# Column-tiled mask, sums and memory selection, an output projection of 512 columns and a Pm in two parts, in a recurrent attention kernel

## Chip, cores and metric

One core of one Trainium2 chip. The metric is the device time of one execution in microseconds (us); lower is better. "Faster" or "slower" is claimed at 2%. All runs here were with a granted TensorE clock of 0.996 to 0.999 of full speed. In the profiles PE is TensorE's matmuls, PEld its weight loads, ACT the scalar engine, DVE the vector engine and POOL GpSimd. Where two kernels are compared, they ran in the same call on the same chip; "ratio" is the mean time of a kernel's fast runs over the mean time of the other's fast runs of the same rounds, so it is not quite the ratio of the medians quoted beside it.

## The reference, cut to what matters

A memory-augmented attention goes through a sequence in 64 segments of 32 rows. Each segment sees 8 memory rows and its own 32 rows, and the first 8 rows of its output are the next segment's memory. So the 64 steps form a chain. (A channel MLP, independent of it, is mixed in at the end.)

```python
for s in range(64):                                   # n_seg
    h = concat([mem, x[:, 32*s:32*s+32]], axis=1)     # 8 + 32 rows, 512 wide
    q, k, v = (einsum('btd,dhe->bhte', h, W) for W in (Wq, Wk, Wv))   # 32 heads of 128
    scores = where(mask, einsum('bhqe,bhke->bhqk', q, k) * scale, -1e9)
    o = einsum('bhqk,bhke->bhqe', softmax(scores), v)
    o = einsum('bhte,hed->btd', o, Wo)                # to 512
    mem = o[:, :8]                                    # the chain
    outs.append(o[:, 8:])
```

## The kernel before

The kernel runs four steps per group of 128 rows of x. I call a step's place in its group its **quarter**, 0 to 3. In each step TensorE makes Q, K, V of the segment (`qk_unit`, `v_unit`), scores, sums for the softmax, the product of the memory rows (`Pm`), the output projection of them (`wo_unit`, together with the previous step's x rows, which lag behind), the mask of the next step, the product of the x rows (`Px`), and the selection of the new memory from the projection's result `wsb`. (`UTT` is the product copied out of PSUM for the projection; `hT` holds the next step's input, transposed.) Between them stand units of *fill*: matmuls of other work (`run_fill`). Eight units of fill are used in quarters 0 to 2: five behind the sums, one before the projection, two behind the selection. In quarter 3 the units are six, one, two *before* the selection and one behind it.

Most of these matmuls use a quarter of the array's columns (`tile_position=(0, 32*j)`): four with different j run side by side. The two products use a quarter of the rows (`(32*j, 0)`). Sums, mask and selection use the whole array.

```python
def mask_mm():
    B = bank(7, [P, 512])
    S = B[:, 0:NG * EW].rearrange("p (i e) -> p i e", e=EW)
    nc.tensor.matmul(S, lhsT=ident[:], rhs=MkA[:].unsqueeze(2).to_broadcast([P, 4, 2, EW]), start=True, stop=True, ...)
    return B, S

def wo_unit(bk, ut, c0, u, d0=0, d1=Dm):
    for (j, i) in HORD[4 * u:4 * u + 4]:
        g = i % 4
        nc.tensor.matmul(bk[32 * g:32 * g + 32, :], lhsT=ut[:, i, j, c0:c0 + 32], rhs=Wo_sb[:, 4 * i + j, d0:d1],
                         start=(j == 0 and i < 4), stop=(j == 3 and i >= NG - 4), tile_position=(0, 32 * g))

# --- in step s, after Q, K, V and scores (cut) ---
nc.scalar.activation(out=E[:, :, 0:16], in_=S[:, :, 0:16], func=ACTF.Exp, scale=scale, accum_out=hist[:, s, 0:1])
nc.scalar.activation(out=E[:, :, 16:EW], in_=S[:, :, 16:EW], func=ACTF.Exp, scale=scale, accum_out=hist[:, s, 1:2])
sm = bank(nc_, [P, NG, 8])
nc.tensor.matmul(sm[:], lhsT=BO[:], rhs=E[:, :, 8:16], start=True, stop=False)
nc.tensor.matmul(sm[:], lhsT=BO[:], rhs=E[:, :, 0:8], start=False, stop=True)
...
run_fill(5 + (si == 3))
nc.vector.reciprocal(out=R[:, 0:8 * NG]..., in_=sm[:])
nc.vector.tensor_tensor(out=Pm..., in0=E[:, :, 0:16]..., in1=R[:, 0:8 * NG]..., op=ALU.mult)      # 128 columns
av(Um, 8, s, V, Pm, 8, 0, 0)                         # 32 matmuls on Pm[.., 8:16], then 8 on Pm[.., 0:8]
nc.tensor.matmul(sr, lhsT=BO[:], rhs=E[:, :, 16:48], ...)                  # row sums, into bank 7
nc.tensor.matmul(sr[:, :, 24:32], lhsT=BO[:], rhs=E[:, :, 48:56], ...)
for j in range(4):                                   # UTT, by ACT and DVE in turn
    (nc.scalar.copy if j % 2 else nc.vector.tensor_copy)(out=UTT[..., j, ...], in_=Um[j][:])
nc.vector.reciprocal(out=R[:, 8 * NG:]..., in_=sr)
run_fill(1)
for half in range(2):
    d = slice(256 * half, 256 * half + 256)
    wp = bank((nb, nd)[half], [P, 256])
    for u in range(8):
        wo_unit(wp, UTT[Tp % 2], 24 - 8 * sp, u, 256 * half, 256 * half + 256)
    ...
    (nc.scalar.copy if half else nc.vector.tensor_copy)(out=wsb[:, d], in_=wp[:])
S_next = mask_mm()
av_x(s - 1, (ne, na, nc_, nb))                       # the Px product
run_fill(2 * (si == 3))
for m in range(KC):                                  # selection of the new memory
    nc.tensor.matmul(aT[:, m, :], lhsT=wsb[:, m * P:(m + 1) * P], rhs=Sel[:, 0:M], start=False, stop=True, ...)
nc.vector.tensor_copy(out=hn[:, :, 0:M], in_=aT)     # hT of the next step; its Q waits for this
for _ in fill: pass
```

Of the kernel before, what the change touches and what calls it, by code (L numbers as in the profile page):

```python
# [23 lines left out]
def kernel(ctx, tc, A_x, A_mem0, A_Wq, A_Wk, A_Wv, A_Wo, A_seg_len, B_x, B_w1, B_b1, B_w2, B_b2, gate_w, out):  # L24
# [327 lines left out]
    def prep_q(s):  # L352
        T, si = divmod(s, SPT)
        nc.gpsimd.tensor_copy(out=QT[:, :, 32:40], in_=QL[T % 2][:, :, LEFT * si:LEFT * si + LEFT])

    def mask_mm():

        B = bank(7, [P, 512])
        S = B[:, 0:NG * EW].rearrange("p (i e) -> p i e", e=EW)
        nc.tensor.matmul(S, lhsT=ident[:], rhs=MkA[:].unsqueeze(2).to_broadcast([P, 4, 2, EW]),  # L360
                         start=True, stop=True, skip_group_check=True)
        return B, S

    def scores(S, s, i0, i1):
# [232 lines left out]
    def run_fill(n):  # L597
        for _ in range(n):
            next(fill, None)
# [21 lines left out]
    for s in range(nseg + 2):  # L621
        T, si = divmod(s, SPT)
        live = s < nseg
        hc, hn = hT[s % NHT], hT[(s + 1) % NHT]
        if live:
            fill = side_work(T, si)
        if si == 1 and T + 2 < NT:
            x_load(T + 2)
        if si == 3 and T + 1 < NT:
            left_v_in(T + 1)  # L630
        if si == 3 and T + 2 < NT:
            x_left(T + 2)
        if live:
            B, S = S_next
            na, nb, nc_, nd, ne = ring
            ring = (nd, ne, na, nc_, nb)
            qk_banks = (na, nb, nc_, nd, ne)
            if s >= 2:
                ux_out(s - 2)
                flush(act_q)  # L640
            if s + 1 < nseg:
                prep_h(s + 1)
            if s >= 1:
                prep_q(s)
                x_mul(s - 1)
            flush(dve_q)
            BANKS = [(0,) + HF[0], (1,) + HF[0], (0,) + HF[1], (1, H // 2, 3 * H // 4), (1, 3 * H // 4, H)]
            for bi, (t, h0, h1) in enumerate(BANKS):
                bk = bank(qk_banks[bi], [P, 512])
                for kc in range(KC):  # L650
                    qk_unit(bk, hc, t, h0, h1, kc)
                Tv = qk_tr(bk, h0, h1)
                dst = QT[:, h0:h1, 0:32] if t == 0 else KT[:, h0:h1, :]
                (nc.gpsimd.tensor_copy if bi == 2 else nc.scalar.copy)(out=dst, in_=Tv)  # L654
            V = cw.tile([P, NG, Dh], BF16, tag="V", name="V")
            Vs[s] = V
            vb0, vb1 = bank(na, [P, 512]), bank(nb, [P, 512])
            for kc in range(KC):
                v_unit(vb0, hc, 0, kc)
            nc.scalar.copy(out=v_out(V, 0), in_=vb0[:])  # L660
            flush(dve_q, 9)
            scores(S, s, 0, 3 * NG // 4)
            v_unit(vb1, hc, 1, 0)
            scores(S, s, 3 * NG // 4, NG)
            for kc in range(1, KC):
                v_unit(vb1, hc, 1, kc)
            E = cw.tile([P, NG, EW], BF16, tag="E", name="E")
            R = cw.tile([P, NG * 40], FP32, tag="R", name="R")
            Es[s], Rs[s] = E, R
            nc.scalar.activation(out=E[:, :, 0:16], in_=S[:, :, 0:16], func=ACTF.Exp, scale=scale, accum_out=hist[:, s, 0:1])  # L670
            nc.scalar.activation(out=E[:, :, 16:EW], in_=S[:, :, 16:EW], func=ACTF.Exp, scale=scale, accum_out=hist[:, s, 1:2])
            sm = bank(nc_, [P, NG, 8])
            nc.tensor.matmul(sm[:], lhsT=BO[:], rhs=E[:, :, 8:16], start=True, stop=False)  # L673
            nc.tensor.matmul(sm[:], lhsT=BO[:], rhs=E[:, :, 0:8], start=False, stop=True)  # L674
            nc.scalar.copy(out=v_out(V, 1), in_=vb1[:])
            run_fill(5 + (si == 3))
            nc.vector.reciprocal(out=R[:, 0:8 * NG].rearrange("p (i q) -> p i q", q=8), in_=sm[:])  # L677
            Pm = cw.tile([P, NG, 16], BF16, tag="Pm", bufs=1, name="Pm")
            nc.vector.tensor_tensor(out=Pm[:].rearrange("p i (a q) -> p i a q", q=8), in0=E[:, :, 0:16].rearrange("p i (a q) -> p i a q", q=8),  # L679
                                    in1=R[:, 0:8 * NG].rearrange("p (i q) -> p i q", q=8).unsqueeze(2).to_broadcast([P, NG, 2, 8]), op=ALU.mult)  # L680
            Um = [bank(k, [P, NG, 8]) for k in (nd, ne, na, nc_)]
            av(Um, 8, s, V, Pm, 8, 0, 0)
            sr = B[:, 0:NG * 32].rearrange("p (i q) -> p i q", q=32)
            nc.tensor.matmul(sr, lhsT=BO[:], rhs=E[:, :, 16:48], start=True, stop=False, skip_group_check=True)  # L684
            nc.tensor.matmul(sr[:, :, 24:32], lhsT=BO[:], rhs=E[:, :, 48:56], start=False, stop=True, skip_group_check=True)
            Tp, sp = divmod(s - 2, SPT)
            for j in range(4):
                (nc.scalar.copy if j % 2 else nc.vector.tensor_copy)(out=UTT[Tp % 2][:, :, j, 24 - 8 * sp:24 - 8 * sp + M], in_=Um[j][:])  # L688
            nc.vector.reciprocal(out=R[:, 8 * NG:].rearrange("p (i q) -> p i q", q=32), in_=sr)  # L689
            run_fill(1)  # L690
        else:
            if s == nseg:
                ux_out(s - 2)
                x_mul(s - 1)
                av_x(s - 1, (ne, na, nc_, 7))
            else:
                ux_out(s - 2)
            flush(dve_q)
            Tp, sp = divmod(s - 2, SPT)
        wsb = cw.tile([P, Dm], BF16, tag="wsb", bufs=9, name="wsb")  # L700
        for half in range(2):
            d = slice(256 * half, 256 * half + 256)
            wp = bank((nb, nd)[half], [P, 256])
            for u in range(8):
                wo_unit(wp, UTT[Tp % 2], 24 - 8 * sp, u, 256 * half, 256 * half + 256)
            if half == 0:
                flush(act_q, 2)
            (nc.scalar.copy if half else nc.vector.tensor_copy)(out=wsb[:, d], in_=wp[:])  # L708
        if s >= 2:
            wsbs[s] = wsb  # L710
        if s + 1 < nseg:
            S_next = mask_mm()
        if live and s >= 1:
            av_x(s - 1, (ne, na, nc_, nb))
        run_fill(2 * (si == 3))
        if s + 1 < nseg:
            aT = S_next[0][:, NG * EW:NG * EW + KC * M].rearrange("p (k m) -> p k m", m=M)
            for m in range(KC):
                nc.tensor.matmul(aT[:, m, :], lhsT=wsb[:, m * P:(m + 1) * P], rhs=Sel[:, 0:M], start=False, stop=True, skip_group_check=True)  # L719
            nc.vector.tensor_copy(out=hn[:, :, 0:M], in_=aT)  # L720
        for _ in fill:
            pass
# [142 lines left out]
```

## Time and profile before

| | before |
|---|---|
| time, median (lowest to highest) | 835.51 us (835.13 to 835.79, 4 runs) |
| one step, median by quarter | 10.94, 11.03, 11.21, 11.46 us |
| end of V to Pm product, by quarter | 1.46, 1.46, 1.50, 1.68 us |
| Pm product to selection | 3.38, 3.38, 3.38, 3.93 us |
| selection to the next Q | 0.63, 0.63, 0.63, 0.54 us |
| Q to end of V | 5.47 to 5.54 us |
| TensorE instructions in the program | 48,500 |

The table divides a step by starts of TensorE's matmuls (medians over the 52 steps from the third group of four to the fifteenth, from the single records of the trace; the end of V is the start of its last matmul plus 0.206). A step is a chain on TensorE, so what a part loses or gains by this table is what the kernel loses or gains. The lines on which this rests are in the prediction.

### The profile page before, as it was taken

To read this page: it belongs to the slowest core of one execution; us is meant where nothing else is said; L and a number is where in the kernel's file an instruction comes from. 1 tells how busy PE (TensorE), PEld (TensorE's weight loads), DVE (VectorE), ACT (ScalarE), POOL (GpSimd) and SP (SyncE) were. 2 spreads that over 40 slices of the span, in tenths; PEclk is the share of its full clock that TensorE was granted. 3 is DMA by queue.
4 is the path that set the end of the run, shared out by engine and by line. 5 is a ranking of instruction groups with operands and counts; after the bars stand their busy time and mean duration, and the time that the engine had idled before them with its cause. 6 is when DMAs were issued, how large, how long until landed. Compare 5 with 4: busy or idle time off the path is not lost.

```text
span 832.9 us, 49239 instructions
## 1 busy us (share of the span) xinstructions
PE 804.7 (97%) x22405; PEld 495.4 (59%) x22417; DVE 501.7 (60%) x1019; ACT 434.0 (52%) x1245; POOL 273.7 (33%) x625
## 2 busy tenths in 40 slices
PE   6999999999999999999999999999999999999886
PEld 4665555665666665566566556656656656665554
DVE  5764256565666566666656565656656665666553
ACT  3555544555455555555554555455555555555552
POOL 8000234242424333332424242434243243424220
PEclk9999999999999999999999999999999999999999
DMA  9791210100000010101010100000010101010000
GB/s 318 253 391 44 87 32 7 28 12 24 15 23 23 17 28 10 37 11 35 10 27 13 35 11 22 23 20 26 12 34 10 36 10 35 5 35 5 10 5 24
DMA packets 38216, 37.64 MB, mean 45 GB/s; under 512 B 13545, under 2 KB 36434, under 8 KB 36466
## 3 DMA queue, kind: packets, MB, share of 16 engines
q1 hardware_dynamic: 37874, 34.31, 12.4%
q8 instruction: 177, 2.90, 1.5%
q14 instruction: 37, 0.30, 0.1%
q0 software_dynamic: 128, 0.13, 0.1%
HBM read 26.03 MB, written 6.29 MB: 39 GB/s over the span
## 4 chain that ended last, share of the span: by engine, by line
PE 93%; DVE 3%; DMA 1%; issue 1%; SPq 1%; ACT 1%; DVEq 0%; ACTq 0%
PE b L211 35%; PE b L233 18%; PE b L222 17%; PE b L384 5%; PE hp L456 4%; PE bp L473 4%; PE b L360 2%; PE b L369 2%; PE b L684 2%; PE b L719 1%; PE b L389 1%; PE b L673 1%; DMA Wo_sb<-in_A_x_dram 1%; PE b L320 1%; PE b L373 0%
## 5 line engine op out<-in xcount | busy, mean ns | idle before, releaser
L217 DVE STREAM_TRANSPOSE Tt<-b 128x512 f32<-128x512 f32 (+1 forms) x384 | 225.6, 613 | 85.5 <-PE b L211 71.8
L211 PEld LDWEIGHTS <-hT 128*32 128x32 bf16 x5120 | 134.7, 97 | 100.0 <-DVE hT L720 15.4
L233 PE MATMUL b<-Wo_sb,UTT 128*32 128x256 bf16 (+1 forms) x4736 | 162.7, 285 | 1.2 <-ACT UTT L619 0.8
L222 PE MATMUL b<-Wv_sb,hT 128*32 128x512 bf16 x2048 | 141.9, 379 | 0.0
L211 PE MATMUL b<-Wq_sb,hT 128*32 128x512 bf16 x2048 | 132.9, 380 | 1.4 <-DVE hT L720 1.4
L211 PE MATMUL b<-Wk_sb,hT 128*32 128x256 bf16 (+1 forms) x3072 | 133.3, 308 | 0.0
L233 PEld LDWEIGHTS <-UTT 128*32 128x32 bf16 x4736 | 121.4, 97 | 19.1 <-ACT UTT L619 1.5
L654 ACT CAST KT<-Tt 128x256 bf16<-128x256 f32 (+1 forms) x192 | 87.1, 476 | 53.6 <-DVE Tt L217 53.6
L605 POOL TENSOR_TENSOR Px<-E,R 128x256 bf16<-128x256 bf16 x64 | 43.0, 672 | 218.7 <-DVE R L689 218.7
L689 DVE RECIPROCAL R<-b 128x256 f32<-128x256 f32 x64 | 112.5, 1757 | 0.0
L654 POOL CAST QT<-Tt 128x512 bf16<-128x512 f32 x64 | 39.1, 611 | 192.6 <-DVE Tt L217 192.6
L619 ACT CAST UTT<-b 128x256 bf16<-128x256 f32 x256 | 76.8, 387 | 23.9 <-PE b L389 23.4
L708 ACT CAST wsb<-b 128x256 bf16<-128x256 f32 x66 | 24.6, 372 | 120.1 <-PE b L233 120.1
L677 DVE RECIPROCAL R<-b 128x64 f32<-128x64 f32 x64 | 35.6, 557 | 79.4 <-PE b L674 79.4
L654 ACT CAST QT<-Tt 128x512 bf16<-128x512 f32 x64 | 39.6, 619 | 66.7 <-DVE Tt L217 66.7
L384 PEld LDWEIGHTS <-V 32*128 32x128 bf16 x4096 | 35.3, 91 | 46.2 <-DVE Pm L679 32.0
L222 PEld LDWEIGHTS <-hT 128*32 128x32 bf16 x2048 | 49.5, 96 | 21.1
L688 ACT CAST UTT<-b 128x64 bf16<-128x64 f32 x128 | 20.9, 215 | 75.2 <-PE b L389 75.2
L461 ACT ACTIVATE hg<-hp,b_sb 128x256 bf16<-128x256 f32 x80 | 37.7, 473 | 38.9 <-PE hp L456 38.9
L456 PE MATMUL hp<-yT,w_sb 128*128 128x256 bf16 (+1 forms) x352 | 53.8, 278 | 2.8 <-ACT hg L461 1.5
L607 POOL TENSOR_TENSOR racc<-racc,R 128x320 f32<-128x320 f32 x64 | 55.5, 867 | 0.0
L720 DVE CAST hT<-b 128x32 bf16<-128x32 f32 x63 | 12.1, 191 | 62.4 <-PE b L719 61.6
(116 smaller groups left out, 1075.2 us busy)
## 6 DMA issues: line engine op xcount, KB each, us to landing
Wv_sb<-in_A_Wv_dram SPq DMA_DIRECT2D x4, 1024.0 KB
Wq_sb<-in_A_Wq_dram SPq DMA_DIRECT2D x4, 1024.0 KB
Wk_sb<-in_A_Wk_dram SPq DMA_DIRECT2D x4, 1024.0 KB
Wo_sb<-in_A_Wo_dram SPq DMA_DIRECT2D x2, 2048.0 KB
vd<-vt SPq DMA_DIRECT2D x32, 128.0 KB
vs<-vd SPq DMA_DIRECT2D x256, 16.0 KB
out_dram<-o SPq DMA_DIRECT2D x16, 128.0 KB
Wo_sb<-in_A_x_dram SPq DMA_DIRECT2D x1, 1024.0 KB
```

Of the source, the lines that this page charges most:

```text
L211: nc.tensor.matmul(bk[32 * j:32 * j + 32, 0:n], lhsT=G[:, kc, :], rhs=W5[t][:, kc, h0:h1, j, :], start=(kc == 0), stop=(kc == KC - 1), til ...
L217: nc.vector.transpose(out=Tt[:, 0:n], in_=bk[:, 0:n])
L222: nc.tensor.matmul(bk[32 * j:32 * j + 32, :], lhsT=G[:, kc, :], rhs=Wv5[:, kc, 4 * vb:4 * vb + 4, j, :], start=(kc == 0), stop=(kc == KC - ...
L233: nc.tensor.matmul(bk[32 * g:32 * g + 32, :], lhsT=ut[:, i, j, c0:c0 + 32], rhs=Wo_sb[:, 4 * i + j, d0:d1], start=(j == 0 and i < 4), stop ...
L384: nc.tensor.matmul(U[j][:, i, :], lhsT=V[q, i, :], rhs=Pt[q, i, c_main:c_main + n], start=(i == 0), stop=False, skip_group_check=True, til ...
L456: nc.tensor.matmul(hp[:rows, :], lhsT=w1_sb[:, kc, fc * P:fc * P + rows], rhs=yTs[blk][:, kc, :], start=(kc == 0), stop=(kc == KC - 1))
L461: nc.scalar.activation(out=hg_[:rows, :], in_=hp[:rows, :], func=ACTF.Gelu_apprx_tanh, bias=b1_sb[:rows, fc:fc + 1], scale=1.0)
L605: nc.gpsimd.tensor_tensor(out=Px[:, :, 0:32], in0=E[:, :, 16:48], in1=Rr, op=ALU.mult)
L607: nc.gpsimd.tensor_tensor(out=racc[:], in0=racc[:], in1=R[:], op=ALU.add)
L619: nc.scalar.copy(out=UTT[T % 2][:, :, j, c0 + M:c0 + 40], in_=U[:])
L654: (nc.gpsimd.tensor_copy if bi == 2 else nc.scalar.copy)(out=dst, in_=Tv)
L689: nc.vector.reciprocal(out=R[:, 8 * NG:].rearrange("p (i q) -> p i q", q=32), in_=sr)
```

## The change

The intent: everything but the two products shall run in 32-column tiling, so that TensorE changes its tiling four times a step instead of nine; the projection shall have half as many matmuls; and Pm shall be ready in its first half earlier, now that the fill before the product ends sooner. Cut to its core (the banks of the last steps, and the place where ACT's queued copies are flushed, which moves from between the halves to before the projection, are left out):

```diff
+    def sums(o, rhs, start, stop):
+        for j in range(4):
+            q = slice(32 * j, 32 * j + 32)
+            nc.tensor.matmul(o[q], lhsT=BO[:, q], rhs=rhs, start=start, stop=stop, skip_group_check=True, tile_position=(0, 32 * j))
+    def mem_out(aT, wsb):
+        for m in range(KC):
+            for c in range(4):
+                nc.tensor.matmul(aT[32 * c:32 * c + 32, m, :], lhsT=wsb[:, m * P + 32 * c:m * P + 32 * c + 32], rhs=Sel[:, 0:M], ..., tile_position=(0, 32 * c))
     def mask_mm():
-        nc.tensor.matmul(S, lhsT=ident[:], rhs=MkA[:]..., ...)
+        for j in range(4):
+            q = slice(32 * j, 32 * j + 32)
+            nc.tensor.matmul(S[q], lhsT=ident[:, q], rhs=MkA[:]..., ..., tile_position=(0, 32 * j))
...
-            ring = (nd, ne, na, nc_, nb)
+            ring = (nb, nd, ne, na, nc_)
...
-            nc.tensor.matmul(sm[:], lhsT=BO[:], rhs=E[:, :, 8:16], start=True, stop=False)
-            nc.tensor.matmul(sm[:], lhsT=BO[:], rhs=E[:, :, 0:8], start=False, stop=True)
+            sums(sm, E[:, :, 8:16], True, False)
+            sums(sm, E[:, :, 0:8], False, True)
...
-            nc.vector.tensor_tensor(out=Pm[:]..., in0=E[:, :, 0:16]..., in1=R[:, 0:8 * NG]..., op=ALU.mult)
+            for c in (8, 0):
+                nc.vector.tensor_tensor(out=Pm[:, :, c:c + 8], in0=E[:, :, c:c + 8], in1=R[:, 0:8 * NG]..., op=ALU.mult)
...  # the row sums sr likewise with sums()
-        for half in range(2):
-            wp = bank((nb, nd)[half], [P, 256])
-            for u in range(8):
-                wo_unit(wp, UTT[Tp % 2], 24 - 8 * sp, u, 256 * half, 256 * half + 256)
-            (nc.scalar.copy if half else nc.vector.tensor_copy)(out=wsb[:, d], in_=wp[:])
+        wp = bank(nb, [P, Dm])
+        for u in range(8):
+            wo_unit(wp, UTT[Tp % 2], 24 - 8 * sp, u)
+        nc.scalar.copy(out=wsb[:], in_=wp[:])
...
-            av_x(s - 1, (ne, na, nc_, nb))
+            av_x(s - 1, (nd, ne, na, nc_))
...
-            for m in range(KC):
-                nc.tensor.matmul(aT[:, m, :], lhsT=wsb[:, m * P:(m + 1) * P], rhs=Sel[:, 0:M], ...)
+            mem_out(aT, wsb)
```

More of the change, by code (lines that the diff above doesn't have):

```diff
@@ L354, in prep_q @@
         nc.gpsimd.tensor_copy(out=QT[:, :, 32:40], in_=QL[T % 2][:, :, LEFT * si:LEFT * si + LEFT])
+    def sums(o, rhs, start, stop):
[5 more added lines that the diff above has]
+            for c in range(4):
+                nc.tensor.matmul(aT[32 * c:32 * c + 32, m, :], lhsT=wsb[:, m * P + 32 * c:m * P + 32 * c + 32], rhs=Sel[:, 0:M],
+                                 start=False, stop=True, skip_group_check=True, tile_position=(0, 32 * c))
     def mask_mm():
@@ L359, in mask_mm @@
         S = B[:, 0:NG * EW].rearrange("p (i e) -> p i e", e=EW)
-        nc.tensor.matmul(S, lhsT=ident[:], rhs=MkA[:].unsqueeze(2).to_broadcast([P, 4, 2, EW]),
-                         start=True, stop=True, skip_group_check=True)
+        for j in range(4):
+            q = slice(32 * j, 32 * j + 32)
+            nc.tensor.matmul(S[q], lhsT=ident[:, q], rhs=MkA[:].unsqueeze(2).to_broadcast([P, 4, 2, EW]),
+                             start=True, stop=True, skip_group_check=True, tile_position=(0, 32 * j))
         return B, S
@@ L678 @@
             Pm = cw.tile([P, NG, 16], BF16, tag="Pm", bufs=1, name="Pm")
-            nc.vector.tensor_tensor(out=Pm[:].rearrange("p i (a q) -> p i a q", q=8), in0=E[:, :, 0:16].rearrange("p i (a q) -> p i a q", q=8),
-                                    in1=R[:, 0:8 * NG].rearrange("p (i q) -> p i q", q=8).unsqueeze(2).to_broadcast([P, NG, 2, 8]), op=ALU.mult)
+            for c in (8, 0):
+                nc.vector.tensor_tensor(out=Pm[:, :, c:c + 8], in0=E[:, :, c:c + 8], in1=R[:, 0:8 * NG].rearrange("p (i q) -> p i q", q=8), op=ALU.mult)
             Um = [bank(k, [P, NG, 8]) for k in (nd, ne, na, nc_)]
@@ L683 @@
             sr = B[:, 0:NG * 32].rearrange("p (i q) -> p i q", q=32)
-            nc.tensor.matmul(sr, lhsT=BO[:], rhs=E[:, :, 16:48], start=True, stop=False, skip_group_check=True)
-            nc.tensor.matmul(sr[:, :, 24:32], lhsT=BO[:], rhs=E[:, :, 48:56], start=False, stop=True, skip_group_check=True)
+            sums(sr, E[:, :, 16:48], True, False)
+            sums(sr[:, :, 24:32], E[:, :, 48:56], False, True)
             Tp, sp = divmod(s - 2, SPT)
@@ L690 @@
             run_fill(1)
+            flush(act_q, 2)
         else:
@@ L694 @@
                 x_mul(s - 1)
-                av_x(s - 1, (ne, na, nc_, 7))
+                av_x(s - 1, (nd, ne, na, nc_))
             else:
@@ L700 @@
         wsb = cw.tile([P, Dm], BF16, tag="wsb", bufs=9, name="wsb")
-        for half in range(2):
-            d = slice(256 * half, 256 * half + 256)
-            wp = bank((nb, nd)[half], [P, 256])
-            for u in range(8):
-                wo_unit(wp, UTT[Tp % 2], 24 - 8 * sp, u, 256 * half, 256 * half + 256)
-            if half == 0:
-                flush(act_q, 2)
-            (nc.scalar.copy if half else nc.vector.tensor_copy)(out=wsb[:, d], in_=wp[:])
+        wp = bank(nb, [P, Dm])
+        for u in range(8):
+            wo_unit(wp, UTT[Tp % 2], 24 - 8 * sp, u)
+        nc.scalar.copy(out=wsb[:], in_=wp[:])
         if s >= 2:
@@ L713 @@
         if live and s >= 1:
-            av_x(s - 1, (ne, na, nc_, nb))
+            av_x(s - 1, (nd, ne, na, nc_))
         run_fill(2 * (si == 3))
@@ L717 @@
             aT = S_next[0][:, NG * EW:NG * EW + KC * M].rearrange("p (k m) -> p k m", m=M)
-            for m in range(KC):
-                nc.tensor.matmul(aT[:, m, :], lhsT=wsb[:, m * P:(m + 1) * P], rhs=Sel[:, 0:M], start=False, stop=True, skip_group_check=True)
+            mem_out(aT, wsb)
             nc.vector.tensor_copy(out=hn[:, :, 0:M], in_=aT)
```

## The prediction

> **What bounds the kernel now.** I read the page first, then the chain of work that ended last, then the time-ordered view of one step of the recurrence at the grain of single rows. The page and the chain name TensorE:
>
> ```profile
> PE 804.7 (97%) x22405; PEld 495.4 (59%) x22417; DVE 501.7 (60%) x1019; ACT 434.0 (52%) x1245; POOL 273.7 (33%) x625
> ...
> PEclk9999999999999999999999999999999999999999
> ...
> PE 93%; DVE 3%; DMA 1%; issue 1%; SPq 1%; ACT 1%; DVEq 0%; ACTq 0%
> ```
>
> The clock is full and TensorE carries 93% of the chain, so 64 steps of about 11 us each are set by the order in which TensorE does its work. The 97% is not useful work only: a matmul's end is modelled, and a busy row hides short holes. So I work with starts. The next lines are TensorE's rows around the sums (L673, L674) of one step, quarter 0 of its group of four:
>
> ```profile
> 418.48 0.60 PE L222 MATMUL b<-Wv_sb,hT 128*32 128x512 bf16 x8
> 418.91 0.33 PE L369 MATMUL b<-QT,KT 128*32 128x40 bf16 x24
> 419.07 0.39 PE L222 MATMUL b<-Wv_sb,hT 128*32 128x512 bf16 x4
> ...
> 419.68 0.61 PE L222 MATMUL b<-Wv_sb,hT 128*32 128x512 bf16 x8
> 420.22 0.20 PE L673 MATMUL b<-E,BO 128*128 128x64 bf16 x1
> 420.25 0.19 PE L674 MATMUL b<-E,BO 128*128 128x64 bf16 x1
> 420.38 0.40 PE L222 MATMUL b<-Wv_sb,GL 128*32 128x512 bf16 x4
> ```
>
> "128*32" is a matmul in 32-column tiling, "128*128" one over the whole array. Four matmuls of a column-tiled group run side by side; a group with 512 columns takes 0.216 us (512 columns at 2.4 GHz are 0.213). Eight V matmuls from 419.68 are two groups and free the array at 420.11, yet the sums start at 420.22: a hole of 0.10. The second sum takes its turn after 0.04, and the fill work (L222 on GL) starts at 420.38 rather than 420.28: again 0.10. At 418.91, where V hands over to scores of the same tiling, there is no hole. What is costly is thus the change of tiling, not the change of operands. The other half of the step:
>
> ```profile
> 421.57 0.36 PE L384 MATMUL b<-Pm,V 32*128 32x8 bf16 x32
> 421.79 0.23 PE L389 MATMUL b<-Pm,VL 32*128 32x32 bf16 x8
> 421.95 0.28 PE L684 MATMUL b<-E,BO 128*128 128x256 bf16 x1
> 422.07 0.19 PE L685 MATMUL b<-E,BO 128*128 128x64 bf16 x1
> 422.19 0.40 PE L222 MATMUL b<-Wv_sb,GL 128*32 128x512 bf16 x4
> 422.37 1.76 DVE L689 RECIPROCAL R<-b 128x256 f32<-128x256 f32 x1
> 422.42 1.92 PE L233 MATMUL b<-Wo_sb,UTT 128*32 128x256 bf16 x64
> 424.27 0.36 PE L360 MATMUL b<-MkA,ident 128*128 128x448 bf16 x1
> 424.39 0.37 ACT L708 CAST wsb<-b 128x256 bf16<-128x256 f32 x1 [1.46 <-PE b L233]
> 424.57 0.37 PE L384 MATMUL b<-Px,V 32*128 32x32 bf16 x32
> 424.95 0.26 PE L719 MATMUL b<-Sel,wsb 128*128 128x8 bf16 x4
> 425.14 0.40 PE L222 MATMUL b<-Wv_sb,GL 128*32 128x512 bf16 x4
> 425.25 0.19 DVE L720 CAST hT<-b 128x32 bf16<-128x32 f32 x1 [0.84 <-PE b L719]
> 425.58 0.39 PE L211 MATMUL b<-Wq_sb,hT 128*32 128x512 bf16 x4
> ```
>
> Following the "rows*columns" field: V, sums, fill, Pm product, row sums, fill, output projection, mask, Px product, selection, fill. That is nine changes of tiling a step, and each costs 0.09 to 0.11: nearly 1 us of 11.
>
> **What the Trainium skill says.** "TensorEngine Tiling (Array Packing)", Key Properties, says that changing the tiling mode drains TensorE, while changing only the tile does not; the trace agrees, with 0.10 us for a change and nothing from V to scores. Its Instruction Overhead section puts about 60 cycles on each matmul however few its columns; here 24 scores matmuls occupy 0.16 us (418.91 to 419.07), 0.026 per group of four, so it is paid once a group and not four times. "TensorE: Matmul & The Clock Gate", Part 3, gives a pack's span as one matmul plus about 4 ns a tile; the trace starts neighbours of a group 3 to 4 ns apart. "Perfetto Trace Analysis", Tensor Engine Instruction, warns that the end of a matmul is computed; hence I use starts.
>
> **The change part by part.** It turns sums, mask and selection to 32-column tiles: four changes a step remain (before and after each of the two products), five go. At 0.10 each that would be 0.5 us a step, 32 us in all. Not all of it reaches the end, so I go through the step.
>
> (a) V to Pm product. Now: 420.11 to 421.57, 1.46 us. After: two sums as two groups of four, 0.03 each by the scores rate; five fill groups, 5 x 0.216 plus 0.02 for the switch of their source, 1.10; one change 0.10; together 1.26. The other path into the product: the sum's result (modelled 0.19) lands at 0.23, the reciprocal starts 0.04 later and takes 0.56, Pm starts 0.10 after it, its first half takes about 0.22 (an estimate from the 64-column copies, 219 ns, against 315 mean for 128 columns) and TensorE sees it 0.05 later: 1.20. Just shorter than 1.26. So 0.20 is saved, and 0.23 in quarter 2, where the product starts some 0.055 after Pm now, that is, waits for it. Splitting Pm is what keeps this path shorter; its second half is read 0.2 later, by the L389 matmuls.
>
> (b) Row sums and projection. Sums of 256 and 64 columns take as long in tiles (0.11 + 0.03); the change behind them goes, so fill ends 0.10 earlier. But the projection needs UTT, copied by DVE and ACT after the product; in the last steps, which have no fill and wait for exactly that, it starts 0.79 after the product's start against 0.85. Saved: 0.06, not 0.10. The projection itself is 8 groups of 0.216 = 1.73 for 16 of 0.109 = 1.75: nothing to speak of, half the instructions notwithstanding.
>
> (c) Projection to selection. The mask needs bank 7, which the long reciprocal L689 reads until 422.37 + 1.76 = 424.13; so it can start at about 424.18 instead of 424.27. Mask, one change and Px product last as now, and selection could start 0.09 earlier. But it now needs all of wsb through ACT: from the projection's start 7 x 0.216 = 1.51 to the last group, 0.39 to its end, 0.05 to ACT, 0.59 for the copy (the V copies of that shape: 579 and 585 ns), 0.05 back: 2.59. Now selection starts 424.95 - 422.42 = 2.53 after the projection. The 0.06 won in (b) is given back, and three changes of tiling around here yield nothing in quarters 0 to 2. In quarter 3 two fill groups stand between product and selection and cover the copy: there 0.09 for the mask and 0.10 for the change are both kept, 0.19.
>
> (d) Selection to projections of Q. 16 matmuls in four groups of 0.025 take 0.10, as four whole ones do; fill follows without a change, which saves 0.085 of 425.58 - 424.95 = 0.63. The rival path, selection's end, the hT copy and back (0.10 + 0.17 + 0.04 + 0.19 + 0.05 = 0.55 less overlap), reaches the same 0.54. Quarter 3, with only one fill group, is already at 0.54: nothing there.
>
> Sum: quarters 0 and 1 save 0.28, quarter 2 0.31, quarter 3 0.39; 1.26 per four steps. Fifteen such groups give 18.9. The last four steps, without fill, save some 0.12 each (earlier sums and half Pm, less the longer wsb copy), 0.5. The projection's copy exposes about 0.3 in the two tail steps, and the ACT copy may be nearer 0.62 (the worst of its shape), which would cost 0.03 in 48 steps. I take 18.5 off: **817.2 us**.
>
> **The rivals.** First, *the wsb copy becomes the bound*: one 512-column ACT copy after the whole projection, instead of two halves of which one is hidden. I have it as break-even; if it takes 0.63, as L311's does, and the mask wait adds to it, three quarters lose 0.05 to 0.10 more, 2.5 to 5 us: 820 to 822. Against it: V's copies, of the same shape from PSUM, take 0.58. Second, *small tiled matmuls are not free*: 27 more a step for sums, mask and selection; should each cost 25 ns on its own instead of each group, 0.7 us a step is added and the kernel is slower, about 860. The scores rows speak against it. Third, *all changes count*: if UTT, reciprocal and copy have more slack than I read, 0.4 a step goes, 810. The reciprocal's 1.76 us and the nearly equal ends at 424.13 and 424.17 (reciprocal, projection) speak against it. Fourth, *Pm stays the bound* because the product waits for both halves: then 1.20 grows to about 1.33 and (a) saves 0.13 instead of 0.20: 821.
>
> **Range and chances.** Rivals one and four move it up by 3 to 5 us, the third down by 7; so 811.5 to 822.5. Two per cent faster is about 819.2, only 2 us above the point, and small waits that I missed are likelier than gains that I missed: faster 0.67, same 0.31, slower 0.02.
>
> **What would show it.** In the profile after: no hole between V, sums and fill; the product (a) starting 1.26 after V's end; mask starting about 0.05 after L689's reciprocal ends and TensorE's idle time before it put down to DVE; TensorE waiting for wsb's ACT copy before selection in three of four steps, not in the fourth; selection to Q 0.54 everywhere. It is wrong if a group of four tiled sums takes more than 0.05, if selection starts more than 2.7 after the projection, or if the change from tiles to rows costs more than 0.11.

## The result, and the profile after

| | before | after |
|---|---|---|
| time, median (lowest to highest) | 835.51 us (835.13 to 835.79) | 825.71 us (825.32 to 825.78) |
| ratio, 95% interval | | 0.9882 [0.9865, 0.9899] |
| one step, median by quarter | 10.94, 11.03, 11.21, 11.46 | 10.78, 10.95, 11.05, 11.22 us |
| end of V to Pm product | 1.463, 1.463, 1.498, 1.679 | 1.321, 1.321, 1.432, 1.537 us |
| Pm product to selection | 3.383, 3.383, 3.382, 3.928 | 3.392, 3.392, 3.392, 3.768 us |
| selection to the next Q | 0.628, 0.628, 0.628, 0.539 | 0.587, 0.588, 0.588, 0.604 us |
| TensorE instructions | 48,500 | 47,708 |

The changed kernel is 1.2% faster: the same, by the 2% rule. The prediction said 817.2 us and 811.5 to 822.5; 9.8 us were won where 18.5 were expected. The page still names TensorE (first the busy times, then the chain):

```profile
PE 792.8 (96%) x22021; PEld 442.6 (54%) x22021; DVE 490.7 (60%) x1017; ACT 447.9 (54%) x1245; POOL 272.8 (33%) x625
...
PE 93%; DVE 3%; ACT 1%; DMA 1%; issue 1%; SPq 1%; DVEq 0%; ACTq 0%
```

The time-ordered view of the changed kernel, a step of quarter 0, the same that the prediction shows of the kernel before. Rows of TensorE, ACT and DVE are shown, others left out. The first number is the start, the second the time covered; the bracket tells how long the engine had been idle and what ended it:

```profile
414.92 0.82 PE L222 MATMUL b<-Wv_sb,hT 128*32 128x512 bf16 x12
...
415.38 0.19 ACT L684 ACTIVATION_READ_ACCUMULATOR E<-b 128x1 f32 x1
415.63 0.24 PE L360 MATMUL b<-E,BO 128*32 128x64 bf16 x8
415.69 1.26 PE L222 MATMUL b<-Wv_sb,GL 128*32 128x512 bf16 x20
416.58 0.36 DVE L694 TENSOR_TENSOR Pm<-E,R 128x64 bf16<-128x64 bf16 x2
416.88 0.36 PE L398 MATMUL b<-Pm,V 32*128 32x8 bf16 x32
...
417.26 0.32 PE L360 MATMUL b<-E,BO 128*32 128x256 bf16 x8
417.41 0.39 PE L222 MATMUL b<-Wv_sb,GL 128*32 128x512 bf16 x4
417.68 1.91 PE L233 MATMUL b<-Wo_sb,UTT 128*32 128x512 bf16 x32
417.71 1.76 DVE L703 RECIPROCAL R<-b 128x256 f32<-128x256 f32 x1
419.51 0.37 PE L374 MATMUL b<-MkA,ident 128*32 128x448 bf16 x4
419.64 0.58 ACT L719 CAST wsb<-b 128x512 bf16<-128x512 f32 x1 [1.39 <-PE b L233]
419.82 0.37 PE L398 MATMUL b<-Px,V 32*128 32x32 bf16 x32
420.28 0.27 PE L365 MATMUL b<-Sel,wsb 128*32 128x8 bf16 x16
420.39 0.60 PE L222 MATMUL b<-Wv_sb,GL 128*32 128x512 bf16 x8
420.68 0.19 DVE L730 CAST hT<-b 128x32 bf16<-128x32 f32 x1 [1.22 <-PE b L365]
420.93 0.40 PE L211 MATMUL b<-Wq_sb,hT 128*32 128x512 bf16 x4
```

The 12 V matmuls (three groups) from 414.92 free the array at 415.57, but the tiled sums start at 415.63: by the medians 0.067 of the old hole of 0.106 is left. Sums to fill, 415.63 to 415.69: no hole, 0.06 for eight tiled matmuls. The product comes 0.10 after the fill's end. Sums to fill before the projection, 417.26 to 417.41: no hole. The projection takes 1.73 plus its tail; the mask starts at 419.51, 0.05 after the reciprocal's end (417.71 + 1.76 = 419.46). The selection starts at 420.28, 0.05 after the wsb copy's end (419.64 + 0.58 = 420.22), although the Px product should have left the array at about 420.10 (an estimate from the kernel before, where the selection starts 0.38 after it, 0.10 of that the change of tiling). Selection to fill: no hole. But DVE's hT copy starts at 420.68, some 0.13 after the selection's modelled end (420.28 + 0.27 = 420.55), where the kernel before had 0.04 (424.95 + 0.26 = 425.21 to 425.25). And Q waits for it: its start at 420.93 is 0.06 after the copy's end, and the fill had ended before.

### The profile page after: what moved, and what is told of

It is laid out like the page before. It is cut to its first block, busy times and chain, and to the rows that moved or that the text cites. A ratio compares the mean times of both kernels' runs of the same rounds, so it can differ in the third digit from the quotient of the medians.

```text
span 824.0 us, 48457 instructions
## 1 busy us (share of the span) xinstructions
PE 792.8 (96%) x22021; PEld 442.6 (54%) x22021; DVE 490.7 (60%) x1017; ACT 447.9 (54%) x1245; POOL 272.8 (33%) x625
## 4 chain that ended last, share of the span: by engine, by line
PE 93%; DVE 3%; ACT 1%; DMA 1%; issue 1%; SPq 1%; DVEq 0%; ACTq 0%
PE b L211 34%; PE b L233 18%; PE b L222 16%; PE b L398 5%; PE hp L470 4%; PE bp L487 4%; PE b L360 3%; PE b L374 2%; PE b L365 2%; PE b L383 2%; PE b L403 1%; DMA Wo_sb<-in_A_x_dram 1%; PE b L387 0%; PE b L324 0%; DVE hT L730 0%
## 5 line engine op out<-in xcount | busy, mean ns | idle before, releaser
L211 PEld LDWEIGHTS <-hT 128*32 128x32 bf16 x5120 | 131.2, 97 | 108.4 <-DVE hT L730 23.7
L233 PE MATMUL b<-Wo_sb,UTT 128*32 128x512 bf16 x2624 | 161.5, 380 | 1.3 <-ACT UTT L633 1.0
L719 ACT CAST wsb<-b 128x512 bf16<-128x512 f32 x66 | 38.6, 585 | 116.6 <-PE b L233 116.6
L233 PEld LDWEIGHTS <-UTT 128*32 128x32 bf16 x2624 | 63.6, 96 | 63.7 <-DVE UTT L702 12.1
L222 PEld LDWEIGHTS <-hT 128*32 128x32 bf16 x2048 | 49.4, 96 | 21.2
```

The lines of the kernel that those rows point to most:

```text
L211: nc.tensor.matmul(bk[32 * j:32 * j + 32, 0:n], lhsT=G[:, kc, :], rhs=W5[t][:, kc, h0:h1, j, :], start=(kc == 0), stop=(kc == KC - 1), til ...
L222: nc.tensor.matmul(bk[32 * j:32 * j + 32, :], lhsT=G[:, kc, :], rhs=Wv5[:, kc, 4 * vb:4 * vb + 4, j, :], start=(kc == 0), stop=(kc == KC - ...
L719: nc.scalar.copy(out=wsb[:], in_=wp[:])
```

## The experiments

Twelve kernels in three calls. All gave correct results. The kernel before ran beside them; its median was 834.99 us in the first call, 836.27 in the second and 834.97 in the third, so between calls the ratio is the better measure, and differences of 0.15% between calls are not read as effects. "Step parts" are medians as in the table above. "Stalls" are counted by one rule in every trace (from 118 us on): intervals between neighbouring matmul starts that are over 0.12 us longer than usual for that place of the step.

| run | time (us, median, lowest to highest) | ratio to before, 95% | stalls |
|---|---|---|---|
| control: the changed kernel | 825.56 (825.36 to 825.61) | 0.9887 [0.9872, 0.9901] | 12, 4.1 us |
| selection whole | 826.18 (826.01 to 826.51) | 0.9895 [0.9880, 0.9909] | 10, 3.8 us |
| projection in halves | 831.29 (830.61 to 833.83) | 0.9963 [0.9950, 0.9976] | 27, 11.9 us |
| first Exp without accumulator | 821.82 (821.57 to 822.91) | 0.9846 [0.9833, 0.9858] | 11, 3.9 us |
| Pm whole | 827.63 (827.39 to 827.89) | 0.9902 [0.9887, 0.9918] | 10, 3.6 us |
| sums whole | 833.46 (832.92 to 833.70) | 0.9970 [0.9956, 0.9983] | 10, 3.5 us |
| mask whole | 825.06 (824.22 to 825.25) | 0.9867 [0.9852, 0.9882] | 12, 4.3 us |
| sums and Pm alone | 827.49 (826.97 to 828.01) | 0.9900 [0.9885, 0.9915] | 20, 6.9 us |
| projection as 64 matmuls, one copy | 834.52 (833.67 to 838.18) | 1.0001 [0.9985, 1.0016] | 29, 11.8 us |
| selection done twice | 835.10 (833.84 to 835.47) | 0.9998 [0.9985, 1.0011] | 14, 4.6 us |
| best: no accumulator, mask whole, GpSimd copies moved | 819.37 (818.71 to 820.07) | 0.9812 [0.9800, 0.9825] | 11, 4.0 us |
| the same, selection whole | 820.67 (820.61 to 821.01) | 0.9831 [0.9818, 0.9844] | 10, 3.8 us |

The kernel before has 12 stalls of 4.6 us by the same count.

### Control

No edit.

> The changed kernel again, as the control of the three that run beside it: 825.7 us, ratio 0.988 to the kernel before.

825.56 us, 0.9887: the result repeats, and its step parts agree with the first trace to 0.01.

### Is the tiled selection late? The selection whole

```diff
-            mem_out(aT, wsb)
+            for m in range(KC):
+                nc.tensor.matmul(aT[:, m, :], lhsT=wsb[:, m * P:(m + 1) * P], rhs=Sel[:, 0:M], start=False, stop=True, skip_group_check=True)
```

> The changed kernel with the memory selection whole again (4 matmuls of 128 columns in place of 16 tiled ones). Theory (16 tiled matmuls hand their result to DVE late): the hT copy starts 0.04 after the last selection matmul's modelled end instead of 0.08 to 0.14; but the change of tiling behind the selection returns, so that fill sets the time from selection to Q: 0.63 against 0.59 in quarters 0 to 2; in quarter 3 the change before it returns too (+0.10) less 0.06 of earlier delivery. Sum: 48 x 0.04 + 16 x 0.03 = 2.4, so 828 us: the tiled selection, meant to save 0.085 + 0.1, saves next to nothing. Rival (the hT copy is late for another reason, such as DVE being busy or the late wsb): delivery stays 0.08 or more, and the whole selection costs 0.1 a step, 832 us.

826.18 us. In the time-ordered view (TensorE's rows, then DVE's), a step of quarter 1:

```profile
431.71 0.26 PE L730 MATMUL b<-Sel,wsb 128*128 128x8 bf16 x4
431.90 0.62 PE L211 MATMUL b<-Wk_sb,GL 128*32 128x512 bf16 x8
```

```profile
432.00 0.19 DVE L731 CAST hT<-b 128x32 bf16<-128x32 f32 x1 [1.11 <-PE b L730]
```

The hole behind the selection is back (0.19 from selection to fill), but the hT copy starts 0.03 after the modelled end. Selection to the hT copy is 0.292 in the median against 0.342 tiled (0.359 in quarter 3). The completion signal that TensorE gives for the selection, as the trace's semaphore events have it, comes 14 ns after the modelled end in the median, against 54 ns tiled (28 to 169). Selection to Q is 0.627 in quarters 0 to 2 and 0.539 in quarter 3, as expected. The time lost was 0.6 us, not 2.4. A regular step did lose 0.03 (0.04 in quarter 3; 10.81 for 10.78 in quarter 0), some 2 us in all; this trace took back 0.7 by fewer and shorter stalls and started its first step 0.3 earlier. Whether the 1,512 fewer TensorE instructions caused either is not shown. So the theory holds that the tiled form delivers late, and the rival (0.1 a step, 832 us) falls. **Tiling the selection is worth next to nothing** (0.03 to 0.04 a step): it takes away a change of tiling and puts a later result in its place.

### Is the wsb copy the bound? The projection in halves

```diff
-        wp = bank(nb, [P, Dm]); 8 x wo_unit(wp, ...); nc.scalar.copy(out=wsb[:], in_=wp[:])
+        for half in range(2):                       # as in the kernel before, with its ring of banks
+            wp = bank((nb, nd)[half], [P, 256])
+            8 x wo_unit(wp, ..., 256 * half, 256 * half + 256)
+            (nc.scalar.copy if half else nc.vector.tensor_copy)(out=wsb[:, d], in_=wp[:])
```

> The changed kernel with the output projection in two halves of 256 columns again, half copied by DVE and half by ACT, and the banks as before. Theory (the selection waits for the one 512-column ACT copy in quarters 0 to 2, 0.07 longer than for the Px product): selection starts 0.68 after the mask instead of 0.76, 48 x 0.07 = 3.4 less, 822.3 us. Rival (half the weight loads and instructions are worth something to TensorE): the halves cost 0.02 a step and what the wait gives is lost elsewhere, 826 to 827 us.

831.29 us: not 3.4 less but 5.7 more. The wait for wsb did go: mask to selection fell from 0.760 to 0.690 in quarters 0 to 2. But selection to the hT copy grew from 0.342 to 0.399 there: the selection, now directly behind the Px product, delivers as late as before. The completion signals show why 0.07 could not be had: the Px product's own four signals come 26 ns apart, the last 0.147 after its modelled end, and the selection's followed the last of them by 0.159 in seven of the nine steps of quarters 0 to 2 looked at. So the regular part of a step gained some 0.01 only. And the 27 stalls are 11.9 us, where the control's 12 are 4.1: 7.8 more. (That the loss is smaller, 5.7, is in part the end of the program: from the last Pm product on this run takes 19.5 us, the control 20.6.) My theory of the wait was right and of no use; the rival, that fewer instructions are worth something, was right in kind. It is tested by itself below.

### What do the sums wait for? The first Exp without its accumulator

```diff
-nc.scalar.activation(out=E[:, :, 0:16], ..., accum_out=hist[:, s, 0:1])
+nc.scalar.activation(out=E[:, :, 0:16], ...)
...  # in x_mul, so that the overflow check keeps its sums:
+        nc.gpsimd.tensor_tensor(out=ea, in0=ea, in1=E[:, :, 0:16], op=ALU.add)
```

> The changed kernel, the first Exp without its accumulated output; the sums that its overflow check needs are kept by one more GpSimd addition a step. Theory (the sums wait not for Exp but for the accumulator read behind it, which ends 0.09 later): the hole of 0.057 between V and the sums closes, 64 x 0.05 = 3.3 less, 822.4 us. Rival (the hole is TensorE's own, from loading BO or from the first tiled sums): it stays and the time is 825.7 us.

821.82 us, 3.7 less than the control, against 3.3 expected. The view of ACT and TensorE, a step of quarter 0:

```profile
414.22 0.28 ACT L688 ACTIVATE E<-b 128x128 bf16<-128x128 f32 x1
```

```profile
413.92 0.82 PE L222 MATMUL b<-Wv_sb,hT 128*32 128x512 bf16 x12
414.57 0.23 PE L360 MATMUL b<-E,BO 128*32 128x64 bf16 x8
414.63 0.60 PE L222 MATMUL b<-Wv_sb,GL 128*32 128x512 bf16 x8
```

V to sums has no hole (413.92 + 3 x 0.216 = 414.57). The hole, 0.067 by the medians, was the read of the accumulator, a second ACT instruction of 0.194 us that starts before the Exp's end and ends 0.09 after it; in the changed kernel the sums start 0.051 after its end in every quarter. Of the 0.067, 0.058 reached the product in quarters 0 and 1 (1.321 to 1.263 from V's end). In quarter 2 nothing was won: there the product is held by Pm (1.432 from sums to product, against 1.263 in quarters 0 and 1).

### Is the split of Pm needed? Pm whole

```diff
-            for c in (8, 0):
-                nc.vector.tensor_tensor(out=Pm[:, :, c:c + 8], ...)
+            nc.vector.tensor_tensor(out=Pm[:]..., ...)       # as in the kernel before
```

> The changed kernel with Pm made in one DVE operation again. Theory (after the change TensorE is ready for the Pm product about when the first half of Pm is, 0.02 of slack): the product starts about 0.05 later in quarters 0 and 1, not in quarter 3 (0.15 of slack), and in quarter 2, where the halves take 0.35 beside a GpSimd copy, it is open: 32 x 0.045 = 1.5 more, 827 us. Rival (fill hides Pm as it did before): no difference, 825.6 us.

827.63 us (0.9902 against 0.9887). Sums to product grew from 1.254 to 1.306 in quarters 0 and 1, from 1.37 to 1.44 in quarter 2, and not at all in quarter 3. As the theory said, and the rival (fill hides it anyway) falls. This rests on the step parts: the time, 1.3 us more by the ratios and 2.1 by the medians, is at the 0.15% that is not read as an effect between calls.

### What are the sums worth? The sums whole

```diff
     def sums(o, rhs, start, stop):
-        for j in range(4): ...tile_position=(0, 32 * j)
+        nc.tensor.matmul(o, lhsT=BO[:], rhs=rhs, start=start, stop=stop, skip_group_check=True)
```

> The changed kernel with all sums whole again (4 matmuls of 128 columns a step for 16 tiled ones); mask, selection, projection and Pm stay changed. Theory (nearly all of the gain is the tiled sums): a change of tiling before the first sums, which hides half of itself in the wait for Exp, one behind them and one before the fill that precedes the projection: 0.14 + 0.05 a step, 12 us more, 837 us, no better than the kernel before. Rival (each of the three tiled parts gives its share): 4 to 5 us more, 830 us.

833.46 us: 7.9 more than the control's median (6.9 by the ratios), between theory (12) and rival (4 to 5). V to product is 1.464 in quarters 0 and 1, as in the kernel before, 0.143 more than in the changed kernel; product to selection is 0.04 more in quarters 0 to 2. My 12 us took these two for every step; but in quarter 2 the slow Pm hides most of it (1.464 against 1.432), and in quarter 3 the later projection is absorbed. So without the tiled sums some three quarters of the gain are gone.

### Does each change of tiling cost its 0.1? The mask whole

```diff
-        for j in range(4): nc.tensor.matmul(S[q], lhsT=ident[:, q], ..., tile_position=(0, 32 * j))
+        nc.tensor.matmul(S, lhsT=ident[:], ..., start=True, stop=True, skip_group_check=True)
```

> The changed kernel with the mask whole again (1 matmul for 4). Theory (the mask waits for the long DVE reciprocal, which ends just when a change of tiling would be over): the mask still starts 0.05 after the reciprocal's end, and the time stays at 825.6 us, within 1 us. Rival (each change of tiling costs its 0.1 wherever it stands): 64 x 0.1 more, 832 us.

825.06 us. The view of TensorE and DVE in a step of quarter 0:

```profile
419.90 0.36 PE L372 MATMUL b<-MkA,ident 128*128 128x448 bf16 x1
```

```profile
418.09 1.76 DVE L701 RECIPROCAL R<-b 128x256 f32<-128x256 f32 x1
```

The reciprocal ends at 419.85 and the mask starts 0.05 later, whole as well as tiled: the change of tiling runs beside a wait that is there in any case. **The tiled mask is worth nothing here**; that each change costs its 0.1 wherever it stands is refuted (832 expected).

### Sums and Pm alone

The kernel before with `sums()` and the split of Pm; mask, selection and projection as before.

> The kernel before with two parts of the change alone: sums in 32-column tiling and Pm in two halves; mask, selection and the projection in halves as before. Theory (these two are the change; the rest gives and takes): 0.12 a step from V to the Pm product and 0.055 from the earlier projection, 64 x 0.175 = 11 off 835, so 824 us, if TensorE's instruction supply holds; with stalls as in the run with the halves (27 of them against 12, some 8 us), up to 830 us. Rival (mask, selection and projection matter for half of the gain): 830 us with no more stalls than before.

827.49 us, ratio 0.9900, with 20 stalls of 6.9 us. V to product is as in the changed kernel (1.321, 1.321, 1.431, 1.537). Two of the five parts of the change thus give 1.0% of its 1.2%, even with stalls that the whole change does not have.

### Do more instructions alone cost time? The projection as 64 matmuls

```diff
-        for u in range(8):
-            wo_unit(wp, UTT[Tp % 2], 24 - 8 * sp, u)
+        for d in (0, 256):
+            for u in range(8):
+                wo_unit(wp[:, d:d + 256], UTT[Tp % 2], 24 - 8 * sp, u, d, d + 256)
         nc.scalar.copy(out=wsb[:], in_=wp[:])
```

> The changed kernel with the projection's 32 matmuls of 512 columns a step as 64 of 256 into the same bank, still copied once by ACT: the same sums, banks and copies, only 64 more TensorE rows a step (51,932 in all against 47,708; the same count as the run with the halves). Theory (TensorE's instruction supply runs dry in a step that is dense in short instructions): holes of 0.15 to 0.4 us in TensorE's stream at places that differ from step to step, about 27 of them against 12, and 6 to 8 us more: 832 us. Rival (the run with the halves lost by its copies or its banks): 826 to 827 us, no more holes.

834.52 us: 9 more than the control, for the same sums, bank and copy, and 29 stalls of 11.8 us. One of them, in TensorE's time-ordered view:

```profile
390.44 0.30 PE L398 MATMUL b<-Px,V 32*128 32x32 bf16 x20
391.44 0.24 PE L398 MATMUL b<-Px,V 32*128 32x32 bf16 x12 [0.70 <-issue]
```

In the middle of 32 matmuls that wait for nothing TensorE stands idle for 0.70 us. When TensorE's records are numbered in the order of their starts, 23 of the 29 stalls stand at number 181 or 182 within a block of 256. (Three more, at 165, 173 and 190, are of another kind: they stand at the scores of three steps where the kernel before has one too, and for two of them the view names the wait, ACT's copy into KT.) In the run with the halves, 23 of 27 stand at 193 or 194. The Trainium skill, "Runtime: NRT & Kernel Launch", Instruction fetch mechanics, says that instructions are fetched in blocks of 256 and that the fetch is mostly hidden. The period agrees; that it is hidden does not, where the projection's 128 instructions, mask, Px product and selection follow at 3 to 14 ns each. The kept traces show the fetch too: their DMA records have a queue of kind "instruction" with 190 transfers here and 174 in the changed kernel, mostly of 16 KB, which took 1.0 us in the median. In all 175 blocks of this run between 118 and 806 us, the instruction at the place of the stalls starts at least 1.24 us after the end of the latest such transfer; behind the 23 stalls it starts 1.24 to 1.59 us after it, elsewhere anywhere from 1.24 to 3.43. The kernel before (162 blocks), the changed kernel (161) and the run with the halves (175) have the same floor, 1.22 to 1.36. So TensorE waits there for an instruction transfer, as far as a floor that is never undercut can show it; what happens in the 1.2 us after its end is not shown. This also corrects the halves above: most of their loss is not theirs but the instructions'.

### Why is the tiled selection late? The selection done twice

```diff
+            mem_out(S_next[0][:, 480:512].rearrange("p (k m) -> p k m", m=M), wsb)     # into columns that nothing reads
             mem_out(aT, wsb)
```

> The changed kernel with the 16 tiled selection matmuls done twice, first into 32 unused columns of the same bank, then as before. Theory (short tiled pairs are taken up every 6 ns but finished more slowly, so a backlog grows with their number): TensorE's completion signal of the last one comes more than 0.1 after its modelled end, against 0.054 in the changed kernel, and the first selection start to the hT copy grows from 0.342 by more than 0.15. Rival (a fixed delay, from the mode or from the Px product ahead): completion stays at 0.03 to 0.06 and the growth is the 0.1 of the added starts. Time: 64 x 0.1 to 0.2 more, 832 to 838 us, part of it possibly stalls from 32 more rows a step.

835.10 us. Selection to the hT copy grew from 0.342 to 0.475 in quarters 1 and 2 and to 0.563 in quarter 0, of which some 0.10 is the sixteen added starts. The completion signal came 87 ns after the modelled end in the median, for 54. In quarter 3, where nothing of the Px product is near, it came 76 ns after the end with 32 matmuls and 82 ns with 16. So there the delay does not grow with the number: the backlog theory falls, and the rival's fixed delay stands, larger than the 0.03 to 0.06 I gave it. In quarters 0 to 2 it did grow, with the Px product just ahead; no run separates the two there. What makes it stays open. (Quarter 0 grew by 0.22: there the signal comes 0.175 after the modelled end in the median. I have no cause for that.) The cost of the run, 9.5 us, is more than 64 x 0.10 and the two added stalls explain: the growth from selection to the hT copy, 0.13 to 0.22 a step with the added starts in it, accounts for most of it.

### A better version, with the mask whole and the GpSimd copies moved

```diff
         if si == 3 and T + 1 < NT:
-            left_v_in(T + 1)                        # GpSimd: VL, 1.05 us
...
                 x_mul(s - 1)
+            if si == 3 and T + 1 < NT:
+                left_v_in(T + 1)                    # and x_left(T + 2) likewise
```

with the edits of the first Exp and of the mask.

> A better version: the changed kernel, the first Exp without accumulator (sums kept by GpSimd), the mask whole, and GpSimd's copies of VL and GL moved behind the Px multiplications of their step so that they do not run beside Pm in quarter 2. Theory: -3.8 from the Exp as measured, 0 to -0.5 from the mask, and 0.1 in one step of four from Pm at 0.23 instead of 0.35, -1.6: 820 us. Rival (the slow Pm of quarter 2 has another cause): Pm stays at 0.35 there and the time is 821.5 us.

819.37 us, ratio 0.9812 [0.9800, 0.9825]: 1.9% faster than the kernel before, which the 2% rule calls unclear, and 0.75% faster than the changed kernel. It answers why Pm was slow in quarter 2: of its three edits only the moved copies can be the cause, since that Pm is no faster in the runs with either of the other two alone (0.40 and 0.36 for its first half, against 0.35). In the changed kernel, views of DVE and of GpSimd in such a step:

```profile
438.26 0.59 DVE L694 TENSOR_TENSOR Pm<-E,R 128x64 bf16<-128x64 bf16 x2
```

```profile
437.50 1.04 POOL L299 COPY VL<-vs 128x1024 bf16<-128x1024 bf16 x1
```

and DVE in the better version, the same place:

```profile
436.44 0.36 DVE L698 TENSOR_TENSOR Pm<-E,R 128x64 bf16<-128x64 bf16 x2
```

The two halves took 0.59 us beside the GpSimd copies (VL from 437.50 to 438.54, and a copy of GL behind it from 438.49) (0.35 for the first alone) and 0.36 away from them; sums to product in quarter 2 fell from 1.432, in the run without the accumulator, to 1.262, the value of quarters 0 and 1. The Trainium skill, "SBUF — State Buffer", Who interferes with whom, says that a DVE instruction with two SBUF inputs contends with a GpSimd instruction that reads SBUF; Pm has two (E and R), and the trace agrees.

### The same, with the selection whole

> The same with the selection whole as well (45,812 TensorE rows): by the earlier run it costs 0.04 a step and gives back some stalls; 820.5 us, equal to the one before within 1 us.

820.67 us, 0.9831: 1.3 us slower than with the tiled selection, a little over the 1 us that I allowed. So of the version with the other waits removed, the tiled selection gives 0.15%.

## Why the prediction was wrong

It was wrong in size: two of its terms, (a) and (d), left out waits. The mechanism, that changes of tiling drain TensorE for 0.10 and that five of nine go, is right: no hole is left between sums, fill and projection or between selection and fill. The point-by-point account, in us saved per four steps (quarters 0 to 3; predicted, then measured by the table):

| part | predicted | measured |
|---|---|---|
| (a) end of V to Pm product | 0.20 + 0.20 + 0.23 + 0.20 = 0.83 | 0.142 + 0.142 + 0.066 + 0.142 = 0.49 |
| (b), (c) Pm product to selection | 0 + 0 + 0 + 0.19 = 0.19 | -0.009 - 0.009 - 0.010 + 0.160 = 0.13 |
| (d) selection to Q | 3 x 0.085 + 0 = 0.255 | 0.041 + 0.040 + 0.040 - 0.065 = 0.06 |
| sum | 1.28 | 0.68 |

0.60 a group of four, over 15 groups, is 9.0 us; the shortfall is 18.5 - 9.8 = 8.7. Of the 0.60, 0.34 lies in (a), 0.20 in (d) and 0.06 in (b) and (c). (The prediction's own sum is 1.26, by rounding; and 18.5 off the 835.51 measured here is 817.0, not 817.2.)

**Step (a), the start of the sums.** The prediction let the sums start at V's end. It never asked what they wait for: it read the hole of 0.10 in the kernel before as drain alone. But ACT's rows there were

```profile
419.76 0.28 ACT L670 ACTIVATE E<-b 128x128 bf16<-128x128 f32 x1
419.93 0.19 ACT L670 ACTIVATION_READ_ACCUMULATOR E<-b 128x1 f32 x1
```

so the read ended at 420.12, the drain (from 420.11) hid the wait behind it, and when the drain went, a hole of 0.067 came to light as wait. The run without the accumulator settles it: no hole, 3.7 us less.

**Step (a), Pm in quarter 2.** The prediction took 0.22 for the first half of Pm in every quarter, from other operations. It was 0.226 in quarters 0 and 1 and 0.351 in quarter 2, beside GpSimd's copies. Moved away, it was 0.225 there too. The fourth rival came nearest, in naming Pm as the bound, but for a reason that does not hold: the product did not wait for both halves.

**Step (d), the delivery of the selection.** The prediction put 0.04 from the selection's modelled end to the hT copy, the value of the whole-array selection, and so had 0.54 to Q. Tiled, it is 0.08 in most steps, 0.10 to 0.14 in others, and the start of Q rests on it in every quarter. In quarter 3, where I saw nothing to win or lose, 0.065 was lost. The run with the selection whole shows the 0.04 again.

**Steps (b) and (c) were right.** The projection starts 0.79 after the product; the mask follows the reciprocal by 0.05; selection is 2.60 after the projection for 2.59; the removed changes around the projection yield nothing in quarters 0 to 2. (The prediction counts three there; by its own rows two go, before the fill and before the mask, while Px product to selection stays a change.) The mask run shows it outright for the one before the mask.

**The projection's halves** were called nothing to speak of. In TensorE's time that was so, but 64 instructions more a step cost 9 us, most of it by stalls (11.8 us for 4.1). This did not enter the sum, since the changed kernel has about as many stalls as the kernel before; it suggests that the projection of 512 columns pays for the instructions that the tiled sums, mask and selection add. The end of the program was mis-sized too: from the last Pm product on it takes 20.5 us for 19.4, where the prediction allowed some 0.3 for the one copy; the run with the halves has 19.5 again. Of the prediction's rivals, the wsb copy was break-even as judged, and small tiled matmuls were indeed nearly free to start. None of the listed signs of error fired, but three of the signs of being right did not come: no hole between V and sums (0.067), the product 1.26 after V's end (1.32), selection to Q 0.54 everywhere (0.59 to 0.60). The first failed step was hidden behind the very thing that the change removed.

What stays open: why the tiled selection's completion comes some 0.04 to 0.07 later than the whole one's, and what the 1.2 us after an instruction transfer are.

## What to carry to other kernels

Before taking away a delay that every step pays, list for the instruction behind it each thing that it waits for, and the time at which that is there: what is ready during the delay looks ready in the old profile and becomes the next wait. Count a removed delay only where the next wait ends earlier: here the same 0.10 was worth all of itself before the fill, less than half before the sums and nothing before the mask. And on an engine fed with instructions of a few ns, count the instructions too.

## What the Trainium skill lacked or had wrong

- "TensorEngine Tiling (Array Packing)", Key Properties, says that a change of tiling drains TensorE, but not for how long: about 0.10 us here (0.106 from V to sums and from fill to the Pm product in the kernel before), and nothing where another wait covers it (mask whole: 825.06 us, tiled: 825.56).
- The same page's 60 cycles for each matmul hold here for a group of four column tiles: 24 matmuls of 40 columns start within 0.16 us, and 16 of 8 columns within 0.11.
- "TensorE: Matmul & The Clock Gate", The cost: per-tile semaphore tail, has about 26 ns for each signal, and the four signals of the Px product come 26 ns apart. Its formula also has 4.7 ns for each tile, an estimate of 14 ns more for four tiles than for one. The single signal of the tiled sums came 18 ns later than that of the whole ones (32 after the modelled end for 14), but that of the tiled selection 40 later (54, 28 to 169, for 14).
- "Runtime: NRT & Kernel Launch", Instruction fetch mechanics, calls the fetch of instruction blocks mostly hidden. In a stream of short tiled matmuls with 51,932 instructions there were 29 stalls of 11.8 us, 23 of them at the same place (number 181 or 182) of a block of 256 and 1.24 to 1.59 us after the end of an instruction transfer; with 47,708 there were 12 of 4.1 us.
- No page was found that says that a consumer of an ACT instruction with an accumulated output can wait for the accumulator's read as well: 0.194 us for the read, which ends some 0.09 after the Exp; the sums start 0.051 after it; 3.7 us of the whole.
